# A searched job order, stores on a second queue, and the last tokens of both halves in one store

## The chip, the cores and the metric

One core of a Trainium2 chip; the four sets of experiments below ran on four chips, so each is read against the kernel before of its own set. The metric is device time in microseconds (us). A run is called slow when it is over 1.5% above the fastest of the same kernel, and fast otherwise. Times are medians over runs; a ratio is the mean time of one kernel's fast runs over the mean of the other's fast runs of the same rounds, so it is not quite the ratio of the medians. The profiled span is about 1.8 us shorter than the same run's device time (152.5 for 154.32 in the kernel before), since it goes from the first to the last instruction.

## The reference, cut to what matters

```python
# x: (8, 4224, 192) float32; weight: (8, 7); w_q, w_k: (192, 64); w_out: (192, 192)
w   = softmax(weight)                        # 7-tap causal convolution per head of 24 columns
y   = conv(x, w)
wq  = y @ w_q;  wk = y @ w_k
W   = 1/8 * einsum('bsd,btd->bst', wq, wk)   # linear attention, no softmax
out = relu(einsum('bst,btd->bsd', W, y)) @ w_out
```

Without a softmax the product is done the cheap way: a 192 x 192 Gram matrix per batch, a small matrix M from it, then two matmuls per token. That leaves 26 MB in and 26 MB out of HBM.

## The kernel before

All eight batches are cut into some 480 jobs, named by letters, and emitted in the order of one string that an offline search found: Y is the convolution as matmuls with a band matrix, T transposes, Q makes queries, G and E the Gram matrix, M the small matrix, Z the hidden tokens with relu, O the output, A one O fused with two Z in a 64-row tiling mode; the other letters are small helper jobs.

```python
GATES = {0: 8, 3: 9, 5: 10, 10: 12, 15: 14}   # store n waits until this load of x has landed
ORDER = ("YYYDYDYDYGTDGGGGYDYYDGTGYYDTGDGGTYTWGGGGGHQGGGTEYYMYDYMQ..." ...)   # cut
CLOCK = {...}      # times that the kernel's own planner uses to give evacuations to engines
```

An evacuation is the copy of a result of TensorE out of its accumulators (`ps` in the traces) into a buffer, by VectorE or ScalarE.

Each batch has 4224 tokens in two halves of 2112. A half is four blocks of 512 tokens and a rest of 64. Blocks of both halves share a buffer of 128 partitions, four tokens in each; the rest puts half h on partitions 64h to 64h + 63. The stores:

```python
if rem:                                           # 64 tokens of each half
    parts = [(at + h * HALF * D, [[D, 64], [1, D]], OUT[64 * h : 64 * h + 64, orr, 0, 0:D])
             for h in range(2)]
elif tail:                                        # last block of the last batch, by quarters
    parts = [(at + q * D, [[4 * D, 128], [HALF * D, 2], [1, D]],
              OUT[:, orr, q // 2, 384 * (q % 2) : 384 * (q % 2) + 384]
              .rearrange("p (h d) -> p h d", h=2))]
else:                                             # 512 tokens of each half, 3072-byte rows
    parts = [(at, [[4 * D, 128], [HALF * D, 2], [1, 4 * D]], OUT[:, orr, :, :])]
for at, dims, src in parts:
    st = P.dma("sp", lambda e, at=at, dims=dims, src=src:
               e.dma_start(bass.AP(out_t, at, dims), src), og[orr], evs + wait)
```

`OUT` is a ring of 8 buffers: block n is evacuated into it only when the store of block n - 8 has landed.

TensorE's code is some 5000 instructions. A helper ends a block of code with a branch to the next one and hints at it beforehand, which is meant to have it read in time: the page of the kernel before counts 19 reads of 16 KB (queue q8, 0.31 MB), and from 24 us on no wait of a matmul is put down to one.

## Time and profile before

| kernel before | |
|---|---|
| device time, 3 runs at first | 153.7 us (153.67 to 154.07) |
| profiled span, granted clock | 152.5 us, 0.993 |
| TensorE busy | 140.1 us, last matmul ends 145.9 |
| last store's last packet | 151.2 us |

6.6 us lie between TensorE's last matmul and the end of the span.

### The profile page before, as it was taken

The page shows a single profiled execution, that of the slowest core. Times are in us where ns is not written, and L with a number is a line of the kernel's source. Part 1 is how long each engine was busy: PE and PEld are TensorE (multiplying, and loading weights), DVE is VectorE, ACT ScalarE, POOL GpSimd, SP SyncE. Part 2 cuts the span into 40 slices and gives each one's busy share as a digit, 9 for nine tenths or more (in the row PEclk, how much of TensorE's full clock was granted, in tenths as well). Part 3 has the DMA queues.
Part 4 walks back from the last instruction along what each step waited for, and adds up shares of the span by engine and source line. Part 5 has one row for each costly group of instructions (what it writes and reads, how often), then busy time and mean ns, then how long its engine had stood idle before and what let it go on. Part 6 is the DMA issues. An engine that isn't in the chain of part 4 may idle for free.

```text
span 152.5 us, 5699 instructions
## 1 busy us (share of the span) xinstructions
PE 140.1 (92%) x2457; PEld 101.3 (66%) x2457; DVE 120.3 (79%) x240; ACT 127.7 (84%) x213; POOL 59.2 (39%) x77
## 2 busy tenths in 40 slices
PE   5986789999999999999999999999999999999920
PEld 1466576876776767677776777678577777766710
DVE  6674899978987987888977859999998977795710
ACT  6456579999998899989979989899898888999930
POOL 7999999989854802554200022030200300000000
PEclk9999999999999999999999999999999999999997
DMA  3999999999999999999999999999999989499896
GB/s 107 254 198 180 190 187 170 195 187 194 191 192 196 212 340 339 289 191 279 342 338 225 192 337 335 318 192 290 408 394 407 377 327 344 172 394 375 307 355 201
DMA packets 49144, 40.88 MB, mean 268 GB/s; under 512 B 37472, under 2 KB 41184, under 8 KB 49120
## 3 DMA queue, kind: packets, MB, share of 16 engines
q0 software_dynamic: 36544, 13.40, 74.3%
q1 hardware_dynamic: 12576, 27.14, 48.9%
q8 instruction: 19, 0.31, 0.7%
q14 instruction: 5, 0.04, 0.1%
HBM read 27.96 MB, written 25.95 MB: 353 GB/s over the span
## 4 chain that ended last, share of the span: by engine, by line
PE 68%; DMA 13%; DVE 8%; POOL 3%; issue 2%; ACT 2%; SPq 1%; ACTq 0%; POOLq 0%
PE ps L207 68%; DMA out_dram<-o_sb 8%; DMA xw<-in_x_dram 5%; DVE y L1029 3%; POOL xw L338 2%; DVE yb L1025 2%; ACT o_sb L1029 1%; DVE qt L1029 1%; DVE zt L1033 1%; DVE zr L1033 1%; DVE m_sb L1035 1%; DVE o_sb L1029 1%; SPq L860 1%; ACT y L1029 1%; ACTq L155 0%
## 5 line engine op out<-in xcount | busy, mean ns | idle before, releaser
L207 PE MATMUL ps<-wo,zt 128*128 128x192 bf16 (+2 forms) x410 | 51.0, 267 | 0.2 <-DVE o_sb L1029 0.2
L1029 ACT COPY o_sb<-ps 128x768 f32<-128x768 f32 (+2 forms) x62 | 46.9, 771 | 4.3 <-PE ps L207 2.4
L1029 ACT CAST y<-ps 128x864 bf16<-128x864 f32 (+6 forms) x48 | 39.0, 835 | 5.5 <-PE ps L207 4.9
L207 PEld LDWEIGHTS ps<-y 128*128 128x128 bf16 (+1 forms) x864 | 35.6, 98 | 12.0 <-issue 2.4
L207 PEld LDWEIGHTS ps<-wo,zt 128*128 128x128 bf16 (+1 forms) x410 | 35.0, 114 | 10.4 <-ACT zt L1032 0.7
L207 PE MATMUL ps<-y 128*128 128x64 bf16 (+1 forms) x864 | 40.2, 193 | 1.0 <-DVE yb L1025 0.6
L1025 DVE STREAM_TRANSPOSE yb<-y 128x576 int32<-128x576 int32 x48 | 35.7, 759 | 0.1
L1029 POOL COPY y<-y 128x1152 bf16<-128x1152 bf16 x11 | 12.6, 1143 | 57.6 <-ACT y L1029 35.0
L207 PE MATMUL ps<-xw,band 128*128 128x432 bf16 (+5 forms) x192 | 32.3, 289 | 2.3 <-DMA xw<-in_x_dram 1.3
L1033 DVE TENSOR_SCALAR zt<-ps 128x512 bf16<-128x512 f32 x45 | 30.0, 680 | 4.6 <-PE ps L207 4.3
L338 POOL DMA_DIRECT2D xw<-in_x_dram x35 | 32.2, 932 | 2.0 <-POOL xw L498 1.1
L207 PE MATMUL ps<-qt,m_sb 128*128 128x512 bf16 (+2 forms) x120 | 30.9, 344 | 0.2 <-DVE qt L1029 0.2
L1032 ACT ACTIVATE zt<-ps 128x512 bf16<-128x512 f32 x51 | 29.8, 605 | 1.3 <-PE ps L207 1.1
L1029 DVE CAST y<-ps 128x864 bf16<-128x864 f32 (+2 forms) x20 | 20.5, 1026 | 4.9 <-PE ps L207 4.3
L207 PEld LDWEIGHTS ps<-xw,band 128*128 128x128 bf16 x192 | 13.6, 99 | 8.4 <-DMA xw<-in_x_dram 1.6
L1029 DVE CAST qt<-ps 128x288 bf16<-128x288 f32 (+1 forms) x32 | 12.2, 424 | 8.1 <-PE ps L207 7.9
L207 PE MATMUL ps<-yb,wq 32*64 32x288 bf16 x768 | 15.2, 284 | 0.5 <-DVE y L1029 0.3
L1029 ACT CAST qt<-ps 128x576 bf16<-128x576 f32 x16 | 10.3, 642 | 4.7 <-PE ps L207 4.0
L207 PEld LDWEIGHTS ps<-yb,wq 32*64 32x64 bf16 x768 | 10.6, 102 | 2.8 <-issue 0.7
L207 PEld LDWEIGHTS ps<-qt,m_sb 128*128 128x128 bf16 (+1 forms) x120 | 9.0, 96 | 4.8 <-ACT qt L1029 0.9
L1029 DVE COPY o_sb<-ps 128x192 f32<-128x192 f32 (+2 forms) x12 | 7.4, 613 | 1.3 <-PE ps L207 1.0
L207 PE MATMUL ps<-warm 128*128 128x256 bf16 (+1 forms) x22 | 6.8, 434 | 1.3 <-DVE warm L389 1.3
(62 smaller groups left out, 66.6 us busy)
## 6 DMA issues: line engine op xcount, KB each, us to landing
out_dram<-o_sb SPq DMA_DIRECT2D x31, 768.0 KB, 7.2
xw<-in_x_dram POOLq DMA_DIRECT2D x14, 432.0 KB, 15.3
xw<-in_x_dram POOLq DMA_DIRECT2D x14, 384.0 KB, 16.7
o_sb<-in_x_dram SPq DMA_DIRECT2D x2, 480.0 KB, 4.7
out_dram<-o_sb SPq DMA_DIRECT2D x16, 48.0 KB, 6.3
out_dram<-o_sb SPq DMA_DIRECT2D x4, 192.0 KB, 2.4
xw<-in_x_dram POOLq DMA_DIRECT2D x2, 240.0 KB, 6.7
xw<-in_x_dram POOLq DMA_DIRECT2D x1, 288.0 KB, 6.9
```

Source lines behind the costliest of these rows:

```text
L207: return self.e.matmul(*a, **k)
L338: return e.dma_start(XW[lo:hi, b % NX, half, c : c + n, :], bass.AP(x_t, at, [[D, hi - lo], [CW * D, n], [1, D]]),)
L860: lambda e, at=at, dims=dims, src=src: e.dma_start(bass.AP(out_t, at, dims), src),
L1025: return e.transpose(o, i)
L1029: return e.copy(o, i) if eng == "act" else e.tensor_copy(o, i)
L1032: return e.activation(o, i, AF.Relu)
L1033: return e.tensor_scalar(o, i, 0.0, None, op0=ALU.max)
L1035: else e.tensor_scalar(o, i, scale, None, op0=ALU.mult))
```

## The change

Its intent: a job order in which blocks of code follow each other with at least the time of one code read between; a tail in which three of the last stores don't queue behind others on SP; and one DMA fewer per batch.

```diff
 GATES = {
-    0: 8, 3: 9, 5: 10, 10: 12, 15: 14,
+    0: 9, 9: 12, 14: 14,
 }
-ORDER = ("YYYDYDYDYGTDGGGGYDYYDGTGYYDTGDGG ..."     # cut
+ORDER = ("YYYDYYDYDDYGGTDGGYYTGYDGTYDQDGGH ..."     # cut
 CLOCK = {
-    "x0": (5.0, 7.5, 8.9, 8.1, 10.0, 11.8, 12.8, 13.6), ...
-    "dma": (377e3, 13.2, 1.6, {"x": 2.2, "o": 1.2}),
+    "x0": (5.0, 7.5, 8.9, 8.1, 10.0, 12.9, 13.3, 14.1), ...
+    "dma": (377e3, 13.2, 1.8, {"x": 2.2, "o": 1.8}),          # "fetch" constants too, cut
 }
             if rem:
-                parts = [(at + h * HALF * D, [[D, 64], [1, D]], OUT[64 * h : 64 * h + 64, orr, 0, 0:D])
-                         for h in range(2)]
+                parts = [(at, [[HALF * D, 2], [D, 64], [1, D]], OUT[:, orr, 0, 0:D])]
...
-                st = P.dma("sp", ..., og[orr], evs + wait)
+                if tail and q:
+                    ends.append((f, og[orr], evs + wait))
+                    st = Op("act", f, ())
+                else:
+                    st = P.dma("sp", f, og[orr], evs + wait)
...
+    for f, grp, deps in ends:
+        P.dma("act", f, grp, deps)
     P.op("sp", lambda e: e.nop(), og)
```

## The prediction

Its sum came to 152.3 us with the merged store on 16 engines and about 165 with it on two, but what two terms rest on has to be said here.

- k stands for the number of DMA engines that a transfer runs on. On the page of the kernel before, SP's queue has 920 packets of 4 bytes (37472 under 512 bytes, less 36544 of q0 and 8 rows of 28 bytes): 57 x 16 for 57 transfers and 8 for the load with 8 rows. The text counts these as semaphore writes and takes their number for k. That the merged store would have k = 2, and with it the +17 us of work and the 12 to 14 us of span, was the author's assumption; no trace of the kernel before shows it.
- The 0.14 us of a fused stretch can be worked out from the trace of the kernel before: the next matmul starts 216 ns after one of 512 columns, 83 after one of 192 and 162 to 163 after one of 384 (medians). Unfused, such a stretch has two, four and two of these: 432 + 332 + 325 ns = 1.09 us, for 0.95.

> **What bounds the kernel now.** I read the page first, then busy time by stretches, then the waits, then the timeline of the end.

> The page gives busy shares and DMA queues:

> ```profile
> PE 140.1 (92%) x2457; PEld 101.3 (66%) x2457; DVE 120.3 (79%) x240; ACT 127.7 (84%) x213; POOL 59.2 (39%) x77
> q0 software_dynamic: 36544, 13.40, 74.3%
> q1 hardware_dynamic: 12576, 27.14, 48.9%
> q8 instruction: 19, 0.31, 0.7%
> ```

> TensorE is the busy engine. The DMA engines are as full: the two data queues add up to 123% of 16 engines' span (packets of the cast loads overlap in time). The code of TensorE comes in 19 reads of 16 KB.

> Busy time by stretches, columns us, PE, PEld, DVE, ACT, POOL, clock, DMA share, GB/s:

> ```profile
> 24.00:145.60 121.60, 120.91 (x2139) 88.84 (x2137) 102.77 (x192) 111.96 (x182) 37.05 (x42) 1.00 1.25 285
> ...
> 32.00:36.00 4.00, 4.00 (x62) 3.00 (x58) 3.38 (x7) 3.86 (x6) 4.00 (x5) 1.00 1.59 190
> ...
> 112.00:116.00 4.00, 4.00 (x83) 2.89 (x83) 3.68 (x8) 3.85 (x6) 0.00 (x0) 1.00 1.04 408
> 124.00:134.00 10.00, 10.00 (x178) 7.84 (x176) 8.20 (x17) 8.73 (x15) 0.00 (x0) 1.00 0.70 264
> 149.00:151.00 2.00, 0.00 (x0) 0.00 (x0) 0.00 (x0) 0.00 (x0) 0.00 (x0) 0.87 1.04 326
> ```

> From 24 to 145.6 us TensorE is idle for only 0.7 us. Loads alone run at 190 GB/s (bytes written; twice that is read, float32 to bf16), stores of 3072-byte rows at 408, stores of 768-byte rows at 326. So the DMA work is 13.40 MB / 190 = 70.5 us, plus 31 stores of 768 KB (24.4 MB / 408 = 59.8 us), plus 1.57 MB of small stores (16 of 48 KB, 4 of 192 KB) / 326 = 4.8 us, plus about 3 us for the first staged loads: **138 us** of the 149 between 2 and 151.2. Slack is found in only one long stretch, 124 to 134 us, at a share of 0.70, so 3 us.

> TensorE's waits in the steady part (us in total, times, longest) and the one store that held up an engine:

> ```profile
> PE ps L207 <- DVE qt L1029: 0.4, 2, 0.2
> PE ps L207 <- DVE o_sb L1029: 0.2, 1, 0.2
> PE ps L207 <- ACT y L1029: 0.2, 1, 0.2
> ...
> 79.97 0.80 ACT L1029 COPY o_sb<-ps 128x768 f32<-128x768 f32 x1 [0.81 <-DMA out_dram<-o_sb]
> ```

> No wait is on code. The closest pair of code edges is at 56.7 and 61.1 us (the times of the conditional branches), with 132 weight loads between, and TensorE is not idle at either.

> The end:

> ```profile
> 145.51 4.12 SPq L860 DMA_DIRECT2D out_dram<-o_sb  x6
> 145.57 0.86 ACT L1029 COPY o_sb<-ps 128x384 f32<-128x384 f32 x2
> ...
> 145.10:148.00 2.90, 1.00 1.03 391
> 148.00:149.00 1.00, 1.00 0.79 237
> 149.00:151.30 2.30, 0.82 0.94 295
> 151.30:152.50 1.20, 0.50 0.00 0
> ```

> (The last four: us, clock, DMA share, GB/s.) The last evacuation ends at 146.44, but six stores are issued one after another on SP until 149.6. That looks like an issue-bound tail. It mostly is not: the DMA engines are full the whole time until 151.2, except for a fifth of the microsecond from 148 to 149.

> [...] The packet count agrees where it can be tested: 7936 rows of 31 large stores, 1024 of 16 rest stores, 1024 of 4 quarters, 1664 of the first loads and 8 of the 8-row conv weights are 11656; 57 other transfers at 16 semaphore writes are 912; 8 more for the weights make 12576, exactly the page's count, where k = 16 for the weights would give 12584. [...] The trace's starts show 0.11 us into and 0.20 us out of the 32-row stage, of which the program has 16 before and after.

> **The change, part by part.**

> *Code blocks apart.* It takes away stalls on code. The trace has none, so worth **0**; at most it guards runs that are not profiled.

> *Job order.* The jobs are the same. Fused stretches (letter A in the order) go from 13 to 15. The timeline has one from 77.97 to 78.81, with its switches 0.95 us; [...] Two times 0.14: **-0.3 us**. Of the waits, matmul starts show four pauses above what columns explain in the steady part: 0.30 at 80.5, 0.32 at 81.3, 0.35 at 107.7, 0.36 at 136.8. The first two follow the store wait shown. A new order removes some and makes others: **0** for the rest. The head (before 24 us) has 3 us of waits on loads and their evacuations; the new order puts two more Y jobs before the first finished Gram matrix: **-0.2**.

> *Gates.* Stores 5 to 8 no longer wait for batch 5's first load, so the buffer awaited at 79.97 is free earlier: **-0.6**. By the load of batch 7, 14 stores have gone out instead of 15, and the one that is left out is small, so that load doesn't move. It has little room: it lands at 103.1 and its first matmul is at 105.35.

> *Last stores on ScalarE's queue.* Three quarters (0.5 us of issue each) no longer queue behind one another on SP. The gain is limited by DMA work left over: the 0.2 us of slack from 148 to 149, and a little at the end: **-0.3**.

> *Last tokens of both halves in one store.* It saves one issue of 0.5 to 1.3 us on SP per batch, off the path. But the DRAM side now has outer sizes 2, 64, 192 against 128 rows in SBUF. [...] Then 128 rows go through two engines, 64 each. A row of 768 bytes takes 768 / (326/16) = 38 ns, so eight stores give these two engines 8 x 64 x 38 ns = 19.3 us instead of 2.4: **+17 us of work on two engines**. All engines have 138 us of 149, so these two would need 155 and can use 3 to 5 us of slack. The span would grow by 12 to 14 us, first as late loads (2 us of room at batch 7), late buffers and waits of TensorE, then as a longer tail.

> **Sums.** If the merged store spreads over 16 engines: -0.3 - 0.2 - 0.6 - 0.3 = -1.4, so 153.7 - 1.4 = **152.3 us**. If it runs on two: -1 + 13, so **about 165 us**.

> **Rivals.** (a) Little changes: the DMA engines stay full and the end moves only with the last stores. For: 138 of 149 us and no code wait. Against: 3 us of DMA slack late show that a better order can feed stores sooner. 151 to 154 us. (b) The two-engine store becomes the bound. [...] Against: the trace tests it only where both sides count 8, not 2 against 128, and someone who timed such a loss would hardly have kept it; that last is judgment[...]. 160 to 168 us. (c) Code was a real limit in unprofiled runs and the better spacing pays. For: 19 reads come as close as 5.8 us, edges as close as 4.4. Against: profiled and unprofiled runs agree within 0.4% and no profiled edge idles. 150 to 151 us.

> **Range and chances.** I give (b) 0.3, (c) 0.05 and (a) the rest. The median lies in (a) near its upper part, 153.0. A range for 8 in 10 has to take in (a) and most of (b): 151.0 to 166.0, which is wide because there are two answers, with little between. Faster by over 2% (below 150.6) 0.06; within 2% 0.64; slower 0.30.

> **What would show each step.** Packets: SP's queue loses 816 (three quarters) and 128 if the merged store is spread, so 11632; with k = 2 it is 11520, and a third data queue shows 816. The 48 KB stores become 8 of 96 KB; landing in over 8 us each, or the DMA share near the end at 2 of 16, means (b). The ACT wait on a store near 80 us should go; under (b) waits on stores and loads grow. In (a) the end of TensorE moves to about 144.5 and the tail from it stays 6.5 to 7 us. I am wrong altogether if TensorE's busy time falls by over 1 us, or waits on code had been hidden in the busy time.

## The result, and the profile after

**163.69 us** (162.67 to 168.12, 4 runs, one of them slow) against 153.88 us for the kernel before in the same rounds. The ratio of fast runs is **1.0608** (95% interval 1.0519 to 1.0696): slower. The output is correct.

The page of the kernel after, busy shares and queues:

```profile
PE 139.1 (86%) x2462; PEld 101.8 (63%) x2462; DVE 120.6 (75%) x237; ACT 127.6 (79%) x216; POOL 59.1 (37%) x77
...
q1 hardware_dynamic: 11520, 26.54, 46.5%
q10 hardware_dynamic: 816, 0.59, 1.2%
q8 instruction: 19, 0.31, 0.7%
```

No engine has more to do. SP's queue has 11520 packets, the count that was predicted for k = 2, not the 11632 for k = 16. By the page's packets under 512 bytes, 632 of them have 4 bytes: 16 for each of 38 transfers, 8 for the one with 8 rows, and 2 for each of the 8 merged stores. The bytes have not changed: 27.14 MB before, 26.54 + 0.59 now.

By stretches (us, PE, PEld, DVE, ACT, POOL, clock, DMA share, GB/s):

```profile
24.00:147.60 123.60, 121.69 (x2146) 89.86 (x2146) 102.92 (x186) 112.32 (x189) 36.92 (x42) 1.00 1.22 271
147.60:153.00 5.40, 0.00 (x0) 0.00 (x0) 0.56 (x1) 0.23 (x1) 0.00 (x0) 0.93 1.03 381
153.00:155.00 2.00, 0.00 (x0) 0.00 (x0) 0.00 (x0) 0.00 (x0) 0.00 (x0) 0.50 0.99 324
155.00:160.00 5.00, 0.00 (x0) 0.00 (x0) 0.00 (x0) 0.00 (x0) 0.00 (x0) 0.50 0.12 35
```

All engines but the DMA engines have been done for 7 us, and the DMA share stands at 0.12: two of sixteen engines, 2 / 16 = 0.125, work off 5 us of rows while fourteen idle. The trace's packet records agree: from 155.5 to 159.5 us one to three packets are in flight at a time, where there are 16 to 18 up to 154.5. At the end of the kernel before, the share was about one until 151.2 us, but for one microsecond at 0.79, and then nothing.

TensorE's waits from 24 us on and, from the list of all waits, the evacuations that waited for a buffer of `OUT` (us in total, times, longest):

```profile
PE ps L207 <- ACT o_sb L1032: 1.5, 1, 1.5
PE ps L207 <- DVE m_sb L1038: 0.8, 1, 0.8
PE ps L207 <- DVE o_sb L1032: 0.3, 1, 0.3
...
ACT o_sb L1032 <- DMA out_dram<-o_sb: 2.0, 1, 2.0
DVE o_sb L1032 <- DMA out_dram<-o_sb: 1.9, 1, 1.9
```

Stores that land late hold their buffers, so the evacuations wait 3.9 us where the kernel before waited 0.8, and TensorE with them. Its last matmul ends at 147.6 instead of 145.9.

The issues of stores, times in ns as min/median/max, after:

```profile
L858 SPq DMA_DIRECT2D out_dram<-o_sb x40: 372/955/7877, 53.1 to 149.6; - x40
```

and before:

```profile
L860 SPq DMA_DIRECT2D out_dram<-o_sb x51: 372/514/2103, 49.0 to 149.1; - x51
```

One issue now takes 7.9 us. SP stands at one store for that long (from 55.9 us), and every store behind it waits too. Why this issue takes so long, no view shows.

### The profile page after: what moved, and what is told of

It reads as the page before. It is cut to its first block, busy times and chain, and to the rows that moved or that the text cites. A ratio compares the mean times of both kernels' runs of the same rounds, so it can differ in the third digit from the quotient of the medians.

```text
span 160.9 us, 5699 instructions
## 1 busy us (share of the span) xinstructions
PE 139.1 (86%) x2462; PEld 101.8 (63%) x2462; DVE 120.6 (75%) x237; ACT 127.6 (79%) x216; POOL 59.1 (37%) x77
## 3 DMA queue, kind: packets, MB, share of 16 engines
q0 software_dynamic: 36544, 13.40, 70.4%
q1 hardware_dynamic: 11520, 26.54, 46.5%
## 4 chain that ended last, share of the span: by engine, by line
PE 68%; DMA 12%; DVE 5%; ACT 3%; POOL 2%; issue 1%; POOLq 0%; DVEq 0%
PE ps L207 68%; DMA out_dram<-o_sb 7%; DMA xw<-in_x_dram 5%; POOL xw L338 2%; DVE y L1032 1%; DVE yb L1028 1%; ACT qt L1032 1%; DVE qt L1032 1%; DVE o_sb L1032 1%; ACT o_sb L1032 1%; ACT y L1032 1%; ACT m_sb L1037 0%; DVE m_sb L1038 0%; DVE gs L1032 0%; DVE zt L1036 0%
## 5 line engine op out<-in xcount | busy, mean ns | idle before, releaser
L207 PE MATMUL ps<-wo,zt 128*128 128x192 bf16 (+2 forms) x414 | 50.7, 266 | 0.0
L1032 ACT COPY o_sb<-ps 128x768 f32<-128x768 f32 (+2 forms) x58 | 43.9, 778 | 5.4 <-PE ps L207 2.5
L1032 ACT CAST y<-ps 128x864 bf16<-128x864 f32 (+6 forms) x53 | 43.2, 838 | 5.1 <-PE ps L207 4.3
L207 PEld LDWEIGHTS ps<-y 128*128 128x128 bf16 (+1 forms) x864 | 35.9, 98 | 10.0 <-issue 1.7
L207 PEld LDWEIGHTS ps<-wo,zt 128*128 128x128 bf16 (+1 forms) x414 | 35.2, 114 | 9.7 <-ACT y L1032 0.4
L207 PE MATMUL ps<-y 128*128 128x64 bf16 (+1 forms) x864 | 40.2, 193 | 0.0
L1036 DVE TENSOR_SCALAR zt<-ps 128x512 bf16<-128x512 f32 x49 | 32.5, 682 | 6.4 <-PE ps L207 6.1
L207 PE MATMUL ps<-xw,band 128*128 128x432 bf16 (+5 forms) x192 | 33.4, 286 | 3.6 <-ACT o_sb L1032 1.5
L207 PE MATMUL ps<-qt,m_sb 128*128 128x512 bf16 (+2 forms) x120 | 30.1, 344 | 1.2 <-DVE m_sb L1038 0.8
L1035 ACT ACTIVATE zt<-ps 128x512 bf16<-128x512 f32 x47 | 27.2, 611 | 1.1 <-PE ps L207 0.8
L207 PEld LDWEIGHTS ps<-xw,band 128*128 128x128 bf16 x192 | 13.4, 97 | 8.2 <-ACT o_sb L1032 1.8
L1032 DVE CAST y<-ps 128x864 bf16<-128x864 f32 (+2 forms) x15 | 15.2, 1011 | 3.8 <-PE ps L207 3.5
L207 PE MATMUL ps<-yb,wq 32*64 32x288 bf16 x768 | 15.6, 284 | 2.2 <-DVE yb L1028 2.2
L1032 DVE CAST qt<-ps 128x288 bf16<-128x288 f32 (+1 forms) x31 | 11.8, 422 | 5.1 <-PE ps L207 4.9
L1032 ACT CAST qt<-ps 128x576 bf16<-128x576 f32 (+1 forms) x17 | 10.5, 624 | 5.6 <-PE ps L207 5.1
L1032 DVE COPY o_sb<-ps 128x768 f32<-128x768 f32 (+2 forms) x16 | 10.9, 682 | 5.1 <-PE ps L207 3.1
L207 PEld LDWEIGHTS ps<-yb,wq 32*64 32x64 bf16 x768 | 10.7, 102 | 4.7 <-issue 2.7
L207 PEld LDWEIGHTS ps<-qt,m_sb 128*128 128x128 bf16 (+1 forms) x120 | 8.8, 96 | 6.1 <-issue 1.3
L207 PE MATMUL ps<-warm 128*128 128x256 bf16 (+1 forms) x23 | 6.2, 411 | 1.3 <-DVE warm L389 1.3
```

The costliest lines, as they stand in the source:

```text
L207: return self.e.matmul(*a, **k)
L1032: return e.copy(o, i) if eng == "act" else e.tensor_copy(o, i)
L1035: return e.activation(o, i, AF.Relu)
L1036: return e.tensor_scalar(o, i, 0.0, None, op0=ALU.max)
```

## The experiments

Each kernel was timed against the kernel before in the same rounds. Kernels are compared only within the same rounds. Kernel before in the four sets: 154.31, 154.01, 154.30 and 154.30 us.

| run | what it is | median us | ratio |
|---|---|---|---|
| e1_two_stores | after, with two stores for the rest | 154.85 | 1.0041 (1.0008 to 1.0075) |
| e2_merge_only | before, with the merged store | 163.78 | 1.0606 (1.0586 to 1.0626) |
| e3_act_only | before, with ScalarE's queue | 154.37 | 1.0003 (0.9988 to 1.0017) |
| e4_order_only | before, with order, gates, constants | 156.39 | 1.0092 (1.0048 to 1.0136) |
| e5_merge_spread | after, merged store on 16 engines | 156.02 | 1.0093 (1.0052 to 1.0133) |
| e6_merge_last | after, 2 engines in batch 7 alone | 157.20 | 1.0226 (1.0184 to 1.0268) |
| e7_merge_not_last | after, 2 engines in batches 0 to 6 | 161.21 | 1.0444 (1.0384 to 1.0504) |
| e8_half_rows | after, half the rows in that store | 156.13 | 1.0117 (1.0066 to 1.0168) |
| e9_spread_fill | e5 with the pause filled | 155.21 | 1.0093 (1.0056 to 1.0131) |
| e10_two_halves | before, last block in two stores | 154.12 | 0.9983 (0.9961 to 1.0004) |
| e11_one_store | before, last block in one store | 153.63 | 0.9969 (0.9948 to 0.9989) |
| e12_gates_only | before, with the new gates | 155.92 | 1.0128 (1.0099 to 1.0157) |

At the 2% that counts as a difference on record, only e2 and e7 are slower, e6 is unclear and all others are the same. What is said below of smaller differences rests on the intervals and on the profiles. Several medians mix two levels of runs, which e4 and e9 explain in part.

### Which part costs it: e1, e2, e3, e4

Theory A: the merged store runs on two DMA engines, which become the bound. Theory B: the new order or gates starve the ring of buffers. Theory C: ScalarE's queue is slow at the end.

**e1_two_stores**, on the kernel after:

```diff
-                parts = [(at, [[HALF * D, 2], [D, 64], [1, D]], OUT[:, orr, 0, 0:D])]
+                parts = [(at + h * HALF * D, [[D, 64], [1, D]], OUT[64 * h : 64 * h + 64, orr, 0, 0:D])
+                         for h in range(2)]
```

> The kernel after, with the last tokens of the two halves again in two stores of 64 rows; all else of the change stays. Theory A (the merged store runs on 2 DMA engines and they are the bound): the loss goes, the sum of the other parts is left, 152.3 us as predicted (151.3 to 153.9), no tail of 0.14 DMA share, SP's queue at 12576 - 816 = 11760 packets. Theory B (the new order or the wider gates starve the store buffers near 92 us): still 160 to 164 us, with the pause near 92. Theory C (ScalarE's queue at the end is slow, its issues took 1.3 us): about 161, still a tail of over 10 us behind TensorE.

The loss is gone: 154.85 us. Theories B and C fall as causes of the 6%, since order, gates and queue are all still in it. But 152.3 did not come either.

**e2_merge_only**, the same lines the other way round, on the kernel before.

> The kernel before, with the merged store alone. Theory A: 160 to 166 us, SP's queue at 12576 - 240 = 12336 packets, a last stretch with a DMA share near 0.13. Theories B and C: 153.5 to 154.5, since order and queue are the old ones.

163.78 us, ratio 1.0606, as the whole change. The merged store alone makes the 6%. That both ratios are 1.06 is partly chance, though: in e2's profile TensorE waits 2.6 us for a late buffer at 93 us, and its granted clock then stands at half from 96.4 to 99.8 us, which costs up to 1.7 us and does not happen in the profile of the kernel after. Packets of SP's queue in e2, then e1:

```profile
q1 hardware_dynamic: 12336, 27.13, 46.9%
```

```profile
q1 hardware_dynamic: 11760, 26.55, 47.4%
```

Both are the counts worked out for k = 2 and k = 16.

**e3_act_only**, the `ends` part of the diff alone, on the kernel before.

> The kernel before, with the last three quarter stores on ScalarE's queue alone. Theory A: the DMA engines are full until the end, so only 0.2 to 0.5 us is won, 153.3 to 153.6 us. If SP's issue times were the bound of the tail: 1.5 us less, 152.3. Theory C: several us more.

Nothing: 1.0003, with 0.2% either way. The tail is not bound by SP's issues, as the full DMA share had said; even the 0.2 us expected doesn't show.

**e4_order_only**: `GATES`, `ORDER` and `CLOCK` of the kernel after, all else of before.

> The kernel before, with the new order, gates and clock constants alone. Theory A: the wait near 80 us goes and two more stretches are fused, 152.5 to 153.2 us (predicted -1.1). Theory B: 160 or more. If code blocks close together had cost something in unprofiled runs: under 152.

A miss. The new order is not 1.1 us faster but slower, and its six runs stand at two levels: 154.50 and 154.84 us at clocks of 0.983 and 0.993, and 156.38 to 156.59 at 0.974 to 0.978. The same two levels are in e1 (four runs at 154.29 to 155.00, two at 156.19 and 156.35).

### Is it the engines or the single store: e5

**e5_merge_spread** keeps one store for both halves, but lays the rows out as token, half instead of half, token:

```diff
-                parts = [(at, [[HALF * D, 2], [D, 64], [1, D]], OUT[:, orr, 0, 0:D])]
+                parts = [(at, [[D, 64], [HALF * D, 2], [1, D]], OUT[:, orr, 0, 0:D])]
...  # the relu writes its columns so that token t of half h comes out on partition 2t + h
-  (lambda bk: [(z[:, 0, 0:128], PS[:, bk, 0:128]),
-               (z[0:64, 1, 0:64], PS[0:64, bk, 128:192]),
-               (z[64:128, 1, 64:128], PS[64:128, bk, 128:192])],
+  (lambda bk: [(z[:, 0, :].rearrange("p (t h) -> p h t", h=2),
+                PS[:, bk, 0:128].rearrange("p (h t) -> p h t", h=2)),
+               (z[0:64, 1, 0:128:2], PS[0:64, bk, 128:192]),
+               (z[64:128, 1, 1:128:2], PS[64:128, bk, 128:192])],
```

> The kernel after with the merged store kept as one store, but with the rows laid out token by token (row 2t + h in SBUF), so that the slowest dimension is 64 in DRAM and 128 in SBUF. Theory A (engines chosen by the slowest dimension): 16 engines again, SP's queue at 11520 + 8 x 14 = 11632 packets, the time of the two-store run: 154.2 to 155.0 us, or 156.2 to 156.6 where the clock falls at 17 us. Rival (one store for both halves is slow for another reason, such as alternating between two regions of DRAM): 160 to 164 us.

Two runs at 154.46 and 154.57, four at 156.02 to 156.07: the levels of the two-store run. SP's queue:

```profile
q1 hardware_dynamic: 11632, 26.55, 46.9%
```

That is 14 more for each of the 8 stores than the 11520 of the kernel after: 16 packets beside its 128 rows, not 2. So one store, the same rows, the same bytes and the same two regions of DRAM; what differs is which dimension comes first, with the rows in SBUF (and the relu's columns) permuted to match. At full clock it costs 154.5 us, and 162.7 with the 2 in front: **8.2 us for the order of two numbers**.

### How the loss adds up: e6, e7, e8

**e6_merge_last** and **e7_merge_not_last** choose the form by batch, on the kernel after:

```diff
+                both = [(at, [[HALF * D, 2], [D, 64], [1, D]], OUT[:, orr, 0, 0:D])]
+                parts = both if b == B - 1 else [        # e7: if b < B - 1
+                    (at + h * HALF * D, [[D, 64], [1, D]], OUT[64 * h : 64 * h + 64, orr, 0, 0:D])
+                    for h in range(2)]
```

> The kernel after with the 2-engine store for the last batch alone, two stores elsewhere. Theory A, by work: 56 more rows of 38 ns on two engines behind all else, +2.1 us over the two-store run, 156.5 to 157.2 us (or 1.75 more with the low clock).

At full clock (the profiled run and one more, both 156.53), 2.0 us over e5's 154.5, the size of the 2.1 us of row time. The profile does not show that all of it is this store: the DMA share falls to 0.16 from 152 to 153 us and two packets at a time are in flight until 153.4, but e9 below has such a remainder at its end with the store spread.

> The kernel after with the 2-engine store for batches 0 to 6, two stores for the last. Theory A: the backlog of the two engines adds up over the batches (7 x 2.1 = 15 us) less the slack they find; with the last batch at +2.1 and all eight at +8.6 over the two-store run, +6 to +7: 160.5 to 162 us. If only the last store counted: 154.5 to 155.

Two runs at 160.05 and two at 162.4: 5.5 to 7.9 us over e5's full-clock runs. It adds up over the batches. These two levels are not those of the order: the profiled run is at the upper one and its clock never fell before the end.

**e8_half_rows**, wrong, writes 32 tokens of each half (the second half's from the wrong rows):

```diff
-                parts = [(at, [[HALF * D, 2], [D, 64], [1, D]], OUT[:, orr, 0, 0:D])]
+                parts = [(at, [[HALF * D, 2], [D, 32], [1, D]], OUT[0:64, orr, 0, 0:D])]
```

> The kernel after with the 2-engine store cut to 32 tokens of each half (the other tokens are not written and the second half's are wrong, on purpose): 32 rows for each of the two engines instead of 64. Extra work on them: (32 - 8) x 38 ns x 8 = 7.3 us instead of 17. If slack absorbs a fixed amount (of the 15 us of the first seven stores 5.5 were seen, so 9.4 were absorbed), the first seven now cost nothing and the last its 0.9 us: 155.0 to 156.0 us at full clock, 1.75 more with the low window. If the cost is proportional to rows: half of 8.2, 158.0 to 159.5.

154.76 and 155.43 us, with 156.82 and 156.88 at the low clock: not half of 8.2, but 0.3 to 0.9 over e5's 154.5 (0.0 to 0.6 if each is taken against the kernel before of its own set). So the two engines have slack for their extra rows, and only what goes beyond it shows. (The run also stores 0.39 MB less, by estimate 1.2 us of all engines at the 326 GB/s of such rows; how much of that shows in its time was not tested.)

### Why the new order doesn't gain: e9 and e12

TensorE around 14 us, busy time by stretches as above, in the kernel before:

```profile
14.00:16.00 2.00, 1.72 (x47) 1.44 (x43) 2.00 (x5) 1.52 (x4) 1.94 (x4) 1.00 1.61 191
16.00:18.00 2.00, 1.37 (x50) 1.23 (x57) 2.00 (x5) 0.84 (x4) 1.72 (x4) 1.00 1.61 195
18.00:20.00 2.00, 2.00 (x74) 1.67 (x51) 1.39 (x5) 1.04 (x3) 1.61 (x3) 1.00 1.59 186
```

and in e4_order_only:

```profile
14.00:16.00 2.00, 0.64 (x14) 0.39 (x10) 2.00 (x4) 1.27 (x3) 1.94 (x4) 1.00 1.60 189
16.00:18.00 2.00, 1.32 (x56) 1.08 (x57) 1.49 (x3) 0.27 (x1) 1.63 (x4) 0.91 1.61 195
18.00:20.00 2.00, 2.00 (x40) 2.00 (x38) 1.63 (x6) 1.53 (x5) 1.70 (x3) 0.50 1.58 185
```

The new order asks for the first Q so early that TensorE waits 2.0 us for the transposes on VectorE. In e4's profile the granted clock then falls to 0.50 at 17.6 us for 3.41 us; half of that is 1.7 us, the distance of the levels. Theory D: the two levels, 1.75 us apart, come from this fall of the granted clock to half for 3.4 us after the pause.

**e9_spread_fill**, on e5:

```diff
         if job.pe:
+            if job.name == ("Q", 0, 0):
+                k = min(held, key=lambda k: banks[k][0])
+                fill(k, 16, banks[k][1])          # matmuls on zeros into a bank that Q overwrites
```

> As the run with the spread merged store, with 16 matmuls on zeros in TensorE's 2.3 us pause at 14.4 us. Theory D [...]: all runs at one level, 154.2 to 154.9 us, clock 0.98 or more, granted clock 1.00 from 16 to 22 us. Rival (the levels come from elsewhere, such as the loads' timing): both levels stay.

(Its words for theory D are cut; the theory is as given above.)

Five of six runs at one level, 154.74 to 155.29 us, clocks 0.981 to 0.989, one at 156.70 with 0.978. In its profile:

```profile
16.00:18.00 2.00, 1.80 (x66) 1.27 (x64) 1.49 (x3) 0.28 (x1) 1.63 (x4) 1.00 1.61 195
18.00:20.00 2.00, 2.00 (x53) 2.00 (x50) 1.97 (x6) 1.87 (x6) 1.70 (x3) 1.00 1.59 186
```

The fall of the clock accounts for the upper level as far as profiles go: the three that were taken at this level (e1, e4, e5) show the fall, and the other four with this order and its pause (after, e6, e7, e8) do not. Where the pause lies fits too. The clock records show one step: until the clock first falls, it is full for 143.36 us in the kernel before and 146.77 in the kernel after, 42.0 and 43.0 times 3.413 us, and the low stretch in e4 is one such step. Cut the time from the start of the clock records into windows of 3.41 us. The window that covers the pause began at 14.2 to 14.8 us in the first three, and matmul records fill 0.39 to 0.44 of it. In the other four the pause was split between two windows, from 12.2 to 13.0 and from 15.6 to 16.4, and the emptier one was filled to 0.47 to 0.50. In all fourteen profiles, from the first rise of the clock until the last matmul, no window filled to 0.47 or more was followed by half clock, and each one filled to 0.44 or less was, the one in e2 (0.29) among them. These shares are rough.

The filler run is weaker evidence. One of its six runs is at the upper level, against 10 of 18 in e1, e4 and e5; with equal chances that would happen about 7 times in 100. And in its profile the windows began at 11.8 and 15.2 us, so the pause would have been split there anyway. The filler is no free gain either: its level lies 0.6 us above the lower one of e5, and why is left open, as is the one run at 156.70.

The rest is in the tail. From 136 us on, in the kernel before:

```profile
136.00:138.00 2.00, 1.80 (x15) 1.08 (x13) 1.90 (x3) 1.83 (x4) 0.00 (x0) 1.00 1.02 393
138.00:145.90 7.90, 7.86 (x104) 5.41 (x102) 4.92 (x11) 7.46 (x13) 0.00 (x0) 1.00 0.92 340
```

and in e9:

```profile
136.00:138.00 2.00, 2.00 (x17) 1.29 (x14) 1.14 (x2) 1.95 (x5) 0.00 (x0) 1.00 0.24 94
138.00:145.70 7.70, 7.61 (x64) 5.34 (x61) 6.01 (x13) 7.45 (x14) 0.00 (x0) 1.00 0.97 373
```

TensorE ends 0.2 us earlier than before (145.7 for 145.9), and from 136 to 138 us the DMA engines have next to nothing to store, 94 GB/s for 393. But this pause is not what moves the end: by the packet records both kernels have stored 23.9 MB by 142 us and 27.1 MB by 151. From 150 to 152 us they move the same, in the kernel before and in e9 (us, clock, DMA share, GB/s):

```profile
150.00:152.00 2.00, 0.62 0.56 177
150.00:152.00 2.00, 0.50 0.57 177
```

What differs comes after that. In e9 some 35 KB are left at 151.05 us, and they go one packet at a time until 152.5 us; the kernel before is done at 151.2. Such a remainder, from the last moment with eight or more packets in flight, lasts 0.65 to 1.4 us in the profiles of the new order with spread or separate stores (e1, e4, e5, e9) and 0.1 to 0.55 us in those of the old order (before, e3, e10, e11, e12). Why it is longer there is open.

**e12_gates_only** tests the step predicted at -0.6:

```diff
-    0: 8, 3: 9, 5: 10, 10: 12, 15: 14,
+    0: 9, 9: 12, 14: 14,
```

> The kernel before with the new gates alone (stores 0 to 8 wait for batch 4's second load, 9 to 13 for batch 6's, 14 on for batch 7's); job order as before, two or three evacuations change their engine because the kernel's own planner is told of the gates. The step predicted -0.6: the ACT wait on a store at 80 us goes, and its two pauses of TensorE with it: 153.5 to 153.8 us where before reads 154.0 to 154.3. If the DMA engines are the bound and take the time back: no wait near 80 and the same time as before.

155.92 us, ratio 1.0128: the gates alone cost 1.6 us with the old order. From the timeline of ScalarE:

```profile
89.26 0.80 ACT L1029 COPY o_sb<-ps 128x768 f32<-128x768 f32 x1 [1.19 <-DMA out_dram<-o_sb]
93.55 0.80 ACT L1029 COPY o_sb<-ps 128x768 f32<-128x768 f32 x1 [1.12 <-DMA out_dram<-o_sb]
```

The wait on a store at 80 us is not removed but moved to 89, 93 and 107 and grown, from 0.8 to 3.0 us in all. With the new order, which makes fewer outputs by then, e4 has no wait on a store at all. So these gates do harm in the old order and none that a profile shows in the new one; the new order with the old gates was not run. (This run changes a few evacuations' engines too, since the planner knows of the gates.)

### A version that beats both: e10 and e11

The tail is bound by the DMA engines, and its last 786 KB go in rows of 768 bytes at 326 GB/s, where rows of 3072 bytes get 408. So fewer, longer stores should help more than earlier ones. Both runs take the kernel before with the spread store of e5; **e10_two_halves** stores the last block in two (rows of 1536 bytes), **e11_one_store** in one:

```diff
-                parts = [(at + q * D, [[4 * D, 128], [HALF * D, 2], [1, D]], ...)]    # 4 times
+                parts = [(at + (q - 3) * D, [[4 * D, 128], [HALF * D, 2], [1, 4 * D]],
+                          OUT[:, orr, :, D * (q - 3) : D * (q + 1)])]                 # once, at q = 3
```

> The kernel before, its order and SP's queue, with the spread merged store and the last tokens' four quarter stores (768-byte rows) made two (1536-byte rows). The end is bound by the DMA engines, so longer rows help and fewer issues close the gap at 148 us: 0.3 for the rows, 0.2 for the gap: 153.4 to 153.8 us where before reads 154.0 to 154.3. If issue or latency bound the end: the same as before or slower, since the first of the two stores starts 0.4 us later.

> As the run with two halves, with one store of 768 KB (3072-byte rows) for the last tokens, issued when the last evacuation is done at 146.5 us; the DMA engines have earlier stores to move until 148.5. 786 KB at 406 GB/s instead of 326 saves 0.5 us, the gap 0.2: 153.3 to 153.7. If it waits too long for its data: 154.5 or more.

e10 is 0.9983, not told from 1, with one slow run left out of it. e11 is 0.9969 (0.9948 to 0.9989): 153.63 us for 154.30. The end of e11 (us, PE, PEld, DVE, ACT, POOL, clock, share, GB/s):

```profile
148.00:149.00 1.00, 0.00 (x0) 0.00 (x0) 0.00 (x0) 0.00 (x0) 0.00 (x0) 0.78 1.04 402
149.00:151.30 2.30, 0.00 (x0) 0.00 (x0) 0.00 (x0) 0.00 (x0) 0.00 (x0) 0.50 0.44 170
```

The microsecond that ran at 237 GB/s before runs at 402, and the last packet is at 150.6. Though its one store is issued only when all its data is ready, at 146.1 us, it ends before the last of the four did. It is a small gain, 0.7 us at the last packet of the profile, and about half of it is not the tail's: TensorE's last matmul also ends 0.3 us earlier (145.5). Nor is the tail's share parted from the spread store, which both runs contain: no run has that store alone on the kernel before.

## Why the prediction was right or wrong

The measured time lies in the range, in the branch that was given 0.3; the point of 153.0 lay in the other branch. That the range held it is owed to its spanning both answers; the mechanism that decided was named, worked out and thought the less likely. By its steps:

- **The merged store runs on two engines: right.** Packet counts of all fourteen kernels fit k to the packet, the share of 0.12 shows two engines at the end, e2 has the whole loss and e5 takes it away by the order of dimensions alone. That it would be two was the author's assumption; these counts show it now. The doubt that someone would not have kept such a loss was no evidence about the chip, and it was what pulled the point off.
- **Its size, +12 to +14 us: too large; 8.2 us at full clock** (9.4 in e2 with the old order, a half-clock window included). The row time fits (e6: 2.0 us for 56 rows, 2.1 expected). The term that was mis-sized is the slack: 3 to 5 us were granted to the two engines, but 17 - 8.2 = 8.8 us of the extra work did not show. The prediction's own figures had 149 - 138 = 11 us that no engine needs. Near 155 us of work after a start at 2 us would end at 157; the last packet is at 159.9, so the two engines ran with some 3 us of idle time in all. e8 shows the same: 7.3 us of extra rows cost under 1.
- **How it would show: right in kind.** Late buffers (3.9 us of evacuations waiting), a later last matmul (1.7 us), then the tail (6.6 us to 13.3). The loads, which the prediction had late first, moved by about 1 us: batch 7's first half landed at 103.8 us for 102.8. With the old order they did come late: at 106.4 in e2.
- **ScalarE's queue, -0.3: about nothing** (e3: 1.0003). The reason given, that the DMA engines are full until the end, was right and left even less.
- **Job order, -0.3, and the head, -0.2: wrong in sign, as far as e4 shows.** At full clock e4's runs, with the gates in them, are 0.2 to 0.5 us slower than before. The prediction counted fused stretches and Y jobs, and did not ask what the early Q would wait for: VectorE's transposes, 2.0 us, with the clock at 0.50 for 3.41 us after it in e4's profile.
- **Gates, -0.6: wrong** (e12: +1.6 with the old order). It removed a wait from the place where it was seen and did not ask where the next buffer would be short.
- **Code blocks, 0: not contradicted.** The profiles of before and after put no wait of TensorE down to the issue of its instructions. Those of e1, e2 and e4 have four or five such pauses, 0.8 to 0.9 us in all; in e1 and e4 two of them, of 0.16 us, lie within 0.4 us of an edge, but that code was the cause is not shown. By the branches' starts the new order's edges are not further apart either: the three closest are 4.3, 4.7 and 4.8 us after, 4.4, 5.7 and 5.9 before. Runs that are not profiled could still differ; no run here separates that.
- **The sum without the store, 152.3: wrong**; e5 at full clock is 154.5.
